# The start-up of a fused Fourier-mixing and gated-FFN kernel: even row sets first, half-width sums, merges last

## The chip, the cores and the metric

One core of a Trainium2 chip runs the whole kernel. The metric is the device time of one execution in microseconds, lower is better. The engines are TensorE (PE; its weight loads are listed as PEld), VectorE (DVE), ScalarE (ACT), GpSimd (POOL) and SyncE (SP), which issues the DMAs.

## The reference

```python
x = np.random.randn(8, 3008, 256).astype(np.float32) * 0.1     # batch, sequence, features
X = np.fft.fft(np.fft.fft(x, axis=1), axis=2).real.astype(np.float32)
t = X.reshape(8 * 3008, 256)                                    # tokens
gate = 1.0 / (1.0 + np.exp(-(t @ w_gate)))                      # w_gate, w_val: 256 x 1536
out = (gate * (t @ w_val)) @ w_out                              # w_out: 1536 x 256
```

The weights come as float64 and are made float32 on the chip.

## The kernel before

The Fourier transform over the sequence is matmuls with cosine and sine tables (`stab`); the one over the features is folded into the gate and value weights: `merge` multiplies a weight piece by the feature DFT table `dt` and leaves `G1` (cosines) and `G2` (sines).

**Rows.** A batch has 3008 rows. By symmetry four of them (`s`, `S - s`, `M + s`, `M - s`, with M = 1504) are folded into each other, so that 128 x 6 numbers `s = 6 p + q` remain: partition p, row set q from 0 to 5. `fold_ops` for batch 0 folds one entry of `SLICES` at a time on VectorE (lines 494 to 583: `point`, `first`, two `across`, two feature sums and a clear).

**Sums.** For batch 0, `half` sums over the six sets into two PSUM banks, `ev` (even q) and `od` (odd q), 377 or 376 columns wide: `blk` 0 are the even frequencies (NE = 377), `blk` 1 the odd ones (NO = 376). Cosines and sines each have both. `places` adds and subtracts `ev` and `od` into `pk` (cosines) and `qk` (sines), which the loop reads in chunks of 252 frequencies. `e_sums` does the same for one feature column (the "E" row), 1 partition wide; its result goes through DRAM (`ed`) and is read back by `e_rows` as `ek`, and its first chunk into `e0`.

**Loop.** For each batch, chunk and hidden tile, step i multiplies `G1` and `G2` with `pk` and `qk` into a PSUM bank `pf` (`front_a`, `front_b`), gates it (`gate_a`, `gate_b`: ScalarE and VectorE) and multiplies with `w_out` (`back`, banks `po`). Three banks of one pool serve `pf` and, in the start-up, sums and merges.

**Weights.** Piece j is loaded (`weight_load`), made float32 by `weight_parts` (ScalarE, lines 382 and 383) and `weight_join` (VectorE 392, 393, 395, then GpSimd 397), and merged by `weight_use` and `merge` (bank `ps`, copies at 417 and 418, small loads `ge` at 420). Pieces 0 and 1 are needed before the first step, 2 and 3 after the first `front_b`, and then one each step (5, 6, 8, ...).

**Order.** It is written out by hand: engines work through their instructions in the order in which the code issues them (`manual_schedule`). All SP loads share one queue; eight completion semaphores go round, so a load is issued when the one eight places before it has landed. Start-up in the code, from line 950: loads; parts and joins 0 and 1; warm-up matmuls on `dt`; merges 0 and 1; then for each slice the fold and the sums; placing; joins 2 and 3; the rest of the sine sums; then the loop. All matmuls are issued at line 133 and told apart by their tiles.

## Time and profile before

| | |
|---|---|
| median of three runs | 1909.43 us (1908.23 to 1909.88) |
| the profiled execution, its own time | 1909.15 us |
| its span in the profile | 1907.4 us |
| TensorE busy | 1895.6 us, 99% of the span |
| VectorE, GpSimd, ScalarE busy | 80%, 81%, 71% |
| granted TensorE clock | 1.00 |
| first `pf` weight load | 32.73 us after the start |

The profile is one execution: each row gives an engine's instructions by source line, with start or total, count and the time of one. "A <- B" names what an engine waited for. The chain of waits is followed back from the last instruction, at each step to what released it. Times in the text are microseconds from the start of the span.

### The profile page before, as it was taken

The page shows a single profiled execution, that of the slowest core. Times are in us where ns is not written, and L with a number is a line of the kernel's source. Part 1 is how long each engine was busy: PE and PEld are TensorE (multiplying, and loading weights), DVE is VectorE, ACT ScalarE, POOL GpSimd, SP SyncE. Part 2 cuts the span into 40 slices and gives each one's busy share as a digit, 9 for nine tenths or more (in the row PEclk, how much of TensorE's full clock was granted, in tenths as well). Part 3 has the DMA queues.
Part 4 walks back from the last instruction along what each step waited for, and adds up shares of the span by engine and source line. Part 5 has one row for each costly group of instructions (what it writes and reads, how often), then busy time and mean ns, then how long its engine had stood idle before and what let it go on. Part 6 is the DMA issues. An engine that isn't in the chain of part 4 may idle for free.

```text
span 1907.4 us, 36057 instructions
## 1 busy us (share of the span) xinstructions
PE 1895.6 (99%) x11836; PEld 1756.6 (92%) x11836; DVE 1520.6 (80%) x3375; ACT 1353.2 (71%) x3235; POOL 1543.4 (81%) x2733
## 2 busy tenths in 40 slices
PE   8999999999999999999999999999999999999999
PEld 5788999999999999999999999999999999999998
DVE  7678888878979778897788878888788777977775
ACT  4777777777777777777777777677767777777775
POOL 2489879987999779997799878999789986877770
PEclk9999999999999999999999999999999999999999
DMA  8446221212022121211211212122120110010001
GB/s 315 120 134 80 71 89 51 72 33 81 21 64 54 31 87 32 62 41 37 89 39 48 45 39 81 40 52 58 30 74 17 36 37 15 15 25 17 15 18 30
DMA packets 197333, 109.33 MB, mean 57 GB/s; under 512 B 134823, under 2 KB 188818, under 8 KB 195354
## 3 DMA queue, kind: packets, MB, share of 16 engines
q1 hardware_dynamic: 196568, 106.50, 21.1%
q8 instruction: 95, 1.56, 0.3%
q14 instruction: 92, 0.75, 0.1%
q10 hardware_dynamic: 546, 0.51, 0.1%
q0 software_dynamic: 32, 0.00, 0.0%
HBM read 71.24 MB, written 47.87 MB: 62 GB/s over the span
## 4 chain that ended last, share of the span: by engine, by line
PE 94%; DMA 2%; SPq 1%; POOL 1%; ACT 1%; DVE 0%; issue 0%; ACTq 0%; POOLq 0%
PE pf L133 49%; PE po L133 41%; PE sum L133 2%; DMA rtab<-in_stab_dram 1%; PE ps L133 1%; POOL sf L824 1%; DMA st<-in_stab_dram 1%; SPq L206 1%; DMA raw<-in_moe_w_val_dram 0%; PE od L133 0%; POOL x L507 0%; SPq L192 0%; SPq L375 0%; PE pe L133 0%; PE ev L133 0%
## 5 line engine op out<-in xcount | busy, mean ns | idle before, releaser
L824 POOL TENSOR_TENSOR sf<-h,sf 128x168 f32<-128x168 f32 (+1 forms) x1104 | 621.0, 582 | 79.5 <-DVE h L818 75.9
L824 POOL TENSOR_TENSOR sf<-h 128x168 f32<-128x168 f32 (+1 forms) x920 | 519.3, 584 | 159.8 <-DVE h L818 158.0
L133 PE MATMUL pf<-qk,G 128*128 128x252 f32 (+1 forms) x2304 | 583.4, 376 | 0.9 <-ACT ae L787 0.8
L133 PE MATMUL pf<-pk,G 128*128 128x252 f32 (+1 forms) x2304 | 582.7, 376 | 0.0
L772 ACT ACTIVATE pf<-ek,ge 128x252 f32<-128x252 f32 (+1 forms) x1142 | 538.2, 471 | 23.2 <-DMA ge<-G 3.0
L133 PE MATMUL po<-sf,wf 128*128 128x168 f32 (+1 forms) x2944 | 508.3, 305 | 0.0
L787 ACT ACTIVATE ae<-pf 128x504 f32<-128x504 f32 (+1 forms) x576 | 338.8, 588 | 218.7 <-PE pf L133 217.2
L133 PEld LDWEIGHTS pf<-pk,G 128*128 128x128 f32 x2304 | 435.9, 190 | 53.3 <-ACT pf L772 1.5
L133 PE MATMUL po<-h,wf 128*128 128x168 f32 (+2 forms) x2584 | 461.3, 307 | 0.0
L133 PEld LDWEIGHTS po<-sf,wf 128*128 128x128 f32 x2944 | 453.4, 190 | 8.0
L818 DVE TENSOR_TENSOR h<-pf,z 128x252 f32<-128x252 f32 (+1 forms) x576 | 240.4, 417 | 274.0 <-ACT pf L815 270.5
L802 DVE TENSOR_TENSOR z<-ae,pf 128x504 f32<-128x504 f32 (+1 forms) x576 | 384.6, 668 | 83.1 <-ACT h L801 79.1
L908 DVE TENSOR_TENSOR c<-c 128x168 f32<-128x168 f32 (+1 forms) x920 | 438.7, 500 | 3.3
L133 PEld LDWEIGHTS pf<-qk,G 128*128 128x128 f32 x2304 | 410.6, 190 | 32.3 <-ACT ae L787 2.1
L133 PEld LDWEIGHTS po<-h,wf 128*128 128x128 f32 x2584 | 410.4, 190 | 17.8 <-issue 0.9
L801 ACT ACTIVATE h<-pf 128x252 f32<-128x252 f32 (+1 forms) x576 | 216.9, 376 | 146.3 <-PE pf L133 129.0
L815 ACT ACTIVATE pf<-z 128x252 f32<-128x252 f32 (+1 forms) x576 | 214.3, 372 | 116.4 <-DVE h L814 114.5
L814 DVE TENSOR_TENSOR h<-h,pf 128x252 f32<-128x252 f32 (+1 forms) x576 | 232.9, 404 | 0.0
L824 POOL TENSOR_TENSOR sf<-sf 128x168 f32<-128x168 f32 (+1 forms) x184 | 101.7, 553 | 14.4
L824 POOL TENSOR_TENSOR sf<-sf,h 128x168 f32<-128x168 f32 (+1 forms) x184 | 110.1, 598 | 0.0
L891 ACT COPY c<-po 128x504 f32<-128x504 f32 (+1 forms) x138 | 78.5, 569 | 0.0
L918 DVE STREAM_TRANSPOSE os<-c 128x256 f32<-128x256 f32 x188 | 76.5, 427 | 0.1
(158 smaller groups left out, 876.4 us busy)
## 6 DMA issues: line engine op xcount, KB each, us to landing
x<-xr SPq DMA_DIRECT2D x14, 1536.0 KB
out_dram<-os SPq DMA_DIRECT2D x376, 56.0 KB
xr<-in_xf_dram SPq DMA_DIRECT2D x105, 128.0 KB
x<-x SPq DMA_DIRECT2D x112, 96.0 KB
xr<-in_xf_dram SPq DMA_DIRECT2D x14, 384.0 KB
ek<-ed SPq DMA_DIRECT2D x40, 126.0 KB
out_dram<-os SPq DMA_DIRECT2D x288, 7.0 KB
xr<-in_xf_dram SPq DMA_DIRECT2D x21, 124.0 KB
```

Source lines behind the costliest of these rows:

```text
L133: nc.tensor.matmul(o, l, r, start=start, stop=stop, skip_group_check=True)
L772: nc.scalar.activation(PF[i][:, g], EK[i // NFT], AF.Copy, scale=ge[:, g, f : f + 1])
L787: nc.scalar.activation(AP[i], PF[i], AF.Copy, scale=2.0)
L801: nc.scalar.activation(H[p][:, fh, 0:n], PF[i][:, 0], AF.Sigmoid)
L802: nc.vector.tensor_tensor(z[:, :, ::-1], AP.pop(i), PF[i], op=ALU.subtract)
L814: nc.vector.tensor_tensor(h[:, fh, 0:n], h[:, fh, 0:n], pf[:, 1], op=ALU.mult)
L815: nc.scalar.activation(pf[:, 0], z[:, 0], AF.Sigmoid)
L818: nc.vector.tensor_tensor(h[:, fh, n:], pf[:, 0], z[:, 1], op=ALU.mult)
L824: nc.gpsimd.tensor_tensor(block(p, dst), block(p, a), block(p, b), op=(ALU.subtract, ALU.add)[op])
L891: (nc.vector.tensor_copy if t == 1 or t == 3 else nc.scalar.copy)(C[0][:, 3 * t * R : 3 * (t + 1) * R], PO[t][:, 0 : 3 * R])
L908: nc.vector.tensor_tensor(t[:, dst * R : (dst + 1) * R], *v, op=(ALU.subtract, ALU.add)[op])
L918: nc.vector.transpose(os_[0][0][:, s, 0:nb, h, :], t[:, c0 : c0 + nb * TB])
```

## The change

- **Loads.** Row sets 4, 0, 2 come first, then 5, 1, 3. Sets 0 and 2 are mixed: even partitions of one go with odd partitions of the other, so each is loaded by two DMAs of 64 partitions (every second one). The tables of the even sets are loaded for 377 columns (H0 to H1) instead of 753, for sets 0 and 2 in the same mixed form (`load_mixed`), for set 4 into two zeroed pieces of `wf`, one with its even and one with its odd partitions (`load_apart`). `dt` moves from ScalarE's DMA queue to SP's, behind the rows; weight pieces 0 and 1 follow it. `load_again`, at step 35 of the loop, loads the cosine tables of the even sets whole, for the joint E sums of batches 1 to 7.
- **Sums.** With the sets mixed, all rows of one sum have the same sign under reversal of the frequencies. `seq_sums` makes two even sums x and y over half the columns, and `unfolded` gets all of them as x + y and, reversed, x - y. `e_first` does so for the E row, with ScalarE copies of y and the odd sums and its unfolded row in `ST[0]`.
- **Order.** `SLICES` are 4, (0, 2), 5, 1, 3. The warm-up is 8 matmuls on a zeroed piece of `wf`. Sums follow the folds; joins and merges of pieces 0 and 1 come after most odd sums, with pieces 2 and 3 behind them. `merge` gets its bank from its caller. The copy of `e0` moves from ScalarE to VectorE. `e_joint` holds what `e_sums` did for the other batches.

The diff, without removed helper bodies and blank lines:

```diff
@@ -188,11 +188,29 @@
     table = const.tile([2, 1], F32, name="table")
     ed = dram.tile([B, NK + 1], F32, name="ed")
-    def load_rows(q, n):
-        nc.sync.dma_start(out=X[0][0:NP, :, q : q + n], in_=xf[0, :, :, q : q + n])
-    def load_table(t, q, n, lo=0, hi=NE + NO):
-        nc.sync.dma_start(out=ST[t][0:NP, q : q + n, lo:hi], in_=stab[:, t, q : q + n, lo:hi])
+    def load_rows(*qs):
+        for q in qs:
+            for ps, r in ((slice(0, NP, 2), q), (slice(1, NP, 2), 2 - q)) if q in (0, 2) else ((slice(0, NP), q),):
+                nc.sync.dma_start(out=X[0][ps, :, q], in_=xf[0, ps, :, r])
+    H0, H1 = NE // 2, NE + NO // 2
+    def load_table(t, q):
+        nc.sync.dma_start(out=ST[t][0:NP, q], in_=stab[:, t, q])
+    def load_mixed(t):
+        for ps, qs in ((slice(0, NP, 2), slice(0, 3, 2)), (slice(1, NP, 2), slice(2, None, -2))):
+            nc.sync.dma_start(out=ST[t][ps, 0:3:2, H0:H1], in_=stab[ps, t, qs, H0:H1])
+    apart = [[wf[:, 2 * t + h].rearrange("p m n -> p (m n)")[:, 6 * WC : 6 * WC + NE] for h in range(2)]
+             for t in range(2)]
+    def load_apart(t):
+        for h in range(2):
+            nc.sync.dma_start(out=apart[t][h][h:NP:2], in_=stab[h::2, t, 4, H0:H1])
+    def load_again():
+        nc.sync.dma_start(out=ST[0][0:NP, 0:NQ:2], in_=stab[:, 0, 0:NQ:2])
     NQ4 = NE // 4 + 1
     TILES = [(g, par, par * HP + g * TB) for g in range(2) for par in range(2)]
@@ -405,11 +423,12 @@
         if w == 2:
             WO[c] = WS.pop(j)
         else:
-            merge(WS.pop(j), w, c, (4, 2, 3)[next(turns) % 3] if j > 1 else None)
-    def merge(ws, g, c, other):
+            merge(WS.pop(j), w, c, HELD.pop(j) if j in HELD else bank("ps", 2 + next(turns) % 3 if j else None))
+    HELD = {}
+    def merge(ws, g, c, ps):
         cs = slice(c * WC, (c + 1) * WC)
-        ps = bank("ps", other)
         for h in range(2):
             for t in range(2):
                 mm(ps[:, h * WC : (h + 1) * WC], dt[:, t, h * HD : (h + 1) * HD], ws[:, t, :],
@@ -482,7 +501,7 @@
     TURN = {}
     MORE = {}
-    SLICES = ((0, 1), (2, 3), (4,), (5,))
+    SLICES = (slice(4, 5), slice(0, 3, 2), slice(5, 6), slice(1, 2), slice(3, 4))
     def fold_ops(b, nq):
         x4 = X.pop(b)
@@ -581,7 +600,7 @@
                     nc.vector.tensor_tensor(to[:, :, :, 1:HD], v[:, :, :, 1:HD], v[:, :, :, D - 1 : HD : -1],
                                             op=op)
                 nc.vector.memset(r[:, :, :, 0:1], 0.0)
-            ops += [lambda q=q: half_rows(slice(q[0], q[-1] + 1)) for q in SLICES]
+            ops += [lambda q=q: half_rows(q) for q in SLICES]
         for blk, (v, r) in enumerate(parts):
             if b and blk:
                 W[b, blk] = v[:, :, HD:D], r[:, :, HD:D]
@@ -592,21 +611,49 @@
     PQE = {}
-    def half(b, w, d, blk, sn, other=None):
-        c0, n = ((0, NE), (NE, NO))[blk]
-        ev, od = [bank(name, other and other[i])[:, 0:n] for i, name in enumerate(("ev", "od"))]
-        def sums(*qs):
-            for q in sorted(qs, key=lambda q: q % 2):
-                mm((ev, od)[q % 2], w(q), ST[int(sn)][0:NP, q, c0 : c0 + n], q < 2, q >= NQ - 2)
-        def then():
-            a = evp.tile([P, NE], F32, name="a", tag="a")[:, 0:n]
-            nc.scalar.copy(a, ev)
-            return lambda: places(d, blk, sn, a, od)
-        return sums, then
+    def unfolded(f, x, y, sn=False):
+        nc.vector.tensor_tensor(f[:, H0:H1], x[:, 0:NE], y, op=ALU.add)
+        two = [t[:, 1:NE].rearrange("p (b n) -> p b n", b=2) for t in ((y, x) if sn else (x, y))]
+        nc.vector.tensor_tensor(f[:, 0 : 2 * H1].rearrange("p (b n) -> p b n", b=2)[:, :, H0 - 1 :: -1], *two,
+                                op=ALU.subtract)
+    def seq_sums(what, x, y, od):
+        d = PQE[0][what]
+        w = [W[0, blk][what] for blk in range(2)]
+        cols = (H0, NE - H0, 0), (NE, NO // 2, NE - H0)
+        turn = {}
+        def add(n, key, o, w, tab, first=True):
+            turn[key] = turn.get(key, 0) + 1
+            mm(o, w, tab, turn[key] == 1 and first, turn[key] == n)
+        def even(*qs):
+            for q in qs:
+                for blk, (lo, n, to) in enumerate(cols):
+                    for h in range(2):
+                        if q == 4 or h == q // 2:
+                            tab = apart[what][h][0:NP, to : to + n] if q == 4 else ST[what][0:NP, q, lo : lo + n]
+                            add(2, (h, blk), (x, y)[h][:, to : to + n], w[blk][:, q], tab, blk == 0)
+        def odd(q, *blks):
+            for blk in blks or range(2):
+                lo, n = ((0, NE), (NE, NO))[blk]
+                add(3, blk + 2, od[blk][:, 0:n], w[blk][:, q], ST[what][0:NP, q, lo : lo + n])
+        def copy():
+            a = evp.tile([P, NE], F32, name="a", tag="a")
+            nc.scalar.copy(a, y[:, 0:NE])
+            return a
+        def join(a):
+            f = hp.tile([P, 6 * WC], F32, name="u", tag="h") if what else wf[:, 0].rearrange("p m n -> p (m n)")
+            unfolded(f, x, a, what)
+            return lambda blk, *ends: places(d, blk, what == 1, f[:, blk * NE : NE + blk * NO],
+                                             od[blk][:, 0 : NE - blk], ends)
+        return even, odd, copy, join
     def places(d, blk, sn, ev, od, ends=(0, 1)):
         if 0 in ends:
@@ -691,53 +734,81 @@
-    E0 = []
-    def e_sums(m=B - 1):
...
+    def e_first():
+        ps = bank("pe")
+        cols = (H0, NE - H0, 0), (NE, NO // 2, NE - H0)
+        turn = {}
+        def add(n, band, blk, o, q, tab, first=True):
+            turn[band, blk] = turn.get((band, blk), 0) + 1
+            mm(ps[band * TB : band * TB + 1, o : o + tab.shape[1]], W[0, blk][2][:, q], tab,
+               turn[band, blk] == 1 and first, turn[band, blk] == n)
+                    if q % 2:
+                        lo, n = ((0, NE), (NE, NO))[blk]
+                        add(3, 2 + blk, blk, 0, q, ST[0][0:NP, q, lo : lo + n])
+                        continue
+                    lo, n, to = cols[blk]
+                    for h in range(2):
+                        if q == 4:
+                            add(2, h, blk, to, q, apart[0][h][0:NP, to : to + n], blk == 0)
+                        elif h == q // 2:
+                            add(2, h, blk, to, q, ST[0][0:NP, q, lo : lo + n], blk == 0)
+        def unfold():
+            er = op.tile([P, NK + 1], F32, name="er", tag="os")[0:1]
+            y, *o = (pool.tile([P, 2 * CH], F32, name=tag, tag=tag)[0:1, 0:NE]
+                     for pool, tag in ((zp, "z"), (zp, "z"), (app, "ae")))
+            for i, t in enumerate((y, *o)):
+                n = NE - i // 2
+                nc.scalar.copy(t[:, 0:n], ps[(i + 1) * TB : (i + 1) * TB + 1, 0:n])
+            f = ST[0][0:1, 4:6].rearrange("p q k -> p (q k)")
+            unfolded(f, ps[0:1], y)
+            def part(*ends):
+                for blk in range(2):
+                    places(er, blk, False, f[:, blk * NE : NE + blk * NO], o[blk][:, 0 : NE - blk], ends)
+                part(1)
+                nc.sync.dma_start(out=ed[0:1], in_=er)
+            part(0)
+            return er, end
+        return sums, unfold
     def e_joint():
...
@@ -950,68 +1021,87 @@
     nc.gpsimd.memset(nil, 0.0)
     nc.scalar.activation(table, nil[:, 0, 0:1], AF.Sigmoid)
     nc.gpsimd.dma_start(out=zero, in_=nil)
-    nc.scalar.dma_start(out=dt, in_=dtab.rearrange("(c p) d -> p c d", p=P))
     load_x(0)
-    for j in range(2):
-        weight_load(j)
-    load_rows(0, 2)
-    load_table(0, 0, 2)
-    load_rows(2, 2)
-    load_table(1, 0, 2, 0, NE)
-    load_table(0, 2, 2)
-    load_rows(4, 1)
-    load_table(0, 4, 1)
+    idle = wf[:, 0].rearrange("p m n -> p (m n)")[:, 0 : P + WC]
+    nc.vector.memset(idle, 0.0)
+    for t in apart:
+        for tab in t:
+            nc.gpsimd.memset(tab, 0.0)
+    load_rows(4, 0, 2)
+    for t in range(2):
+        load_apart(t)
+    for t in range(2):
+        load_mixed(t)
     load_rows(5, 1)
-    weight_load(2)
-    load_table(1, 2, 2, 0, NE)
-    load_table(0, 5, 1)
-    load_table(1, 4, 2, 0, NE)
-    load_table(1, 0, NQ, NE)
-    for j in (3, 5, 6, 8, 9, 4, 7):
+    load_table(0, 5)
+    load_rows(3)
+    load_table(0, 1)
+    load_table(1, 1)
+    nc.sync.dma_start(out=dt, in_=dtab.rearrange("(c p) d -> p c d", p=P))
+    weight_load(0)
+    load_table(0, 3)
+    weight_load(1)
+    load_table(1, 5)
+    load_table(1, 3)
+    for j in (2, 3, 5, 6, 8, 9, 4, 7):
         weight_load(j)
     e0 = shared["qk"][:, 4 * WC : 4 * WC + CH]
     nc.gpsimd.memset(e0, 0.0)
+    warm = bank("warm", 2)
+    for i in range(8):
+        mm(warm[:, 0:WC], idle[:, 0:P], idle[:, P:], True, True)
+    seq_start(0)
+    folds = iter(fold_ops(0, 2))
+    even, odd, copy, join = seq_sums(0, bank("u"), bank("u"), [bank("od", t) for t in range(2)])
+    e_, e_unfold = e_first()
+    od_s = [bank("od", 4)]
+    even_s, odd_s, copy_s, join_s = seq_sums(1, bank("u", 2), bank("u", 3), od_s)
+    for q in ((4,), (0, 2)):
+        next(folds)()
+        even(*q)
+        even_s(*q)
+    a, a_s = copy(), copy_s()
+    next(folds)()
+    odd(5)
+    e_(0, 2, 4, 5)
+    for f in folds:
+        f()
+    pk = join(a)
     weight_parts(0)
+    weight_join(0)
+    HELD[0] = bank("ps")
+    od_s.append(bank("od"))
+    odd(1)
+    odd_s(1, 1, 0)
+    e_(1, 3)
+    odd(3)
+    odd_s(5)
     weight_parts(1)
-    weight_join(0)
     weight_join(1)
-    warm = bank("warm", 2)
-    for i in range(4):
-        mm(warm[:, 0:WC], dt[:, 0, 0:P], dt[:, 0], True, True)
+    er, e_end = e_unfold()
+    weight_parts(2)
     weight_use(0)
+    odd_s(3, 1)
+    qk = join_s(a_s)
+    for blk in range(2):
+        pk(blk, 0)
+    nc.vector.tensor_copy(e0[0:1], er[:, 0:CH])
+    HELD[1] = bank("ps", 3)
     weight_use(1)
-    seq_start(0)
-    cos = [seq_group(0, blk, 0, (2 * blk, 2 * blk + 1)) for blk in range(2)]
-    e_, e_even = e_sums(1)
-    sin = [seq_group(0, 0, 1)]
-    for q, f in zip(SLICES, fold_ops(0, 2), strict=True):
-        f()
-        e_(*{1: (0, 1), 5: (2, 3, 4, 5)}.get(q[-1], ()))
-        sin[0][0](*{5: (3,)}.get(q[-1], ()))
-        cos[0][0](*q)
-        cos[1][0](*q)
-        sin[0][0](*{1: (0, 1), 4: (2,), 5: (4, 5)}.get(q[-1], ()))
-    places_c = [cos[blk][1]() for blk in range(2)]
-    weight_parts(2)
+    odd_s(3, 0)
     weight_join(2)
-    rest, *ends = e_even()
-    rest()
-    for f in ends:
-        f()
-    for f in places_c:
-        f()
-    nc.scalar.copy(e0[0:1], E0[0][:, 0:CH])
+    qk(0, 0)
+    qk(1, 0, 1)
     weight_parts(3)
     weight_join(3)
-    sin.append(seq_group(0, 1, 1, (0, 1)))
-    sin[1][0](*range(NQ))
+    qk(0, 1)
+    for blk in range(2):
+        pk(blk, 1)
+    e_end()
     for j in range(KEEP, KEEP + 3):
         weight_load(j)
-    places_s = [group[1]() for group in sin]
-    for f in places_s:
-        f()
     e_rows(0)
     per = NFT * len(chunks)
@@ -1043,6 +1133,7 @@
     for i, f in zip((1, 2, 2, 2, 3, 4, 4, 4, 5, 6, 6, 8, 8, 8, 9, 9, 9, 9, 10, 10, 10, 11, 11), quarter_x(1), strict=True):
         at(i, f)
     at(i0 + 1, lambda: load_x(1))
+    at(35, load_again)
     for b in range(1, B):
         at(20 + b, lambda b=b: e_load(b))
     at(3 * i0, e_fold)
```

## The prediction

> **What bounds the kernel now.** I read the page's totals, then the chain of waits, then the timeline of the first 60 us by engine.
>
> ```profile
> span 1907.4 us, 36057 instructions
> PE 1895.6 (99%) x11836; PEld 1756.6 (92%) x11836; DVE 1520.6 (80%) x3375; ACT 1353.2 (71%) x3235; POOL 1543.4 (81%) x2733
> ```
>
> TensorE is idle for 11.8 us in all. The chain of waits over the first 90 us says where:
>
> ```profile
> 14.43 9.31 DMA st<-in_stab_dram
> 23.74 0.04 issue
> 23.78 0.90 PE ev L133 x2
> ...
> 31.32 1.90 PE od L133 x6
> 33.21 4.25 PE pf L133 x20
> 37.46 3.45 PE ps L133 x16
> 40.91 0.90 PE pf L133 x4
> 41.81 1.73 PE ps L133 x8
> ```
>
> Up to 23.74 us the chain hangs on loads; from there on it is TensorE back to back. So the time is "when the loop's first steps start" plus a fixed amount of matmul, and the change touches only that start-up (after it, the instruction order is the same on every engine, apart from one reload). It can win at most a few us in 1909, and only if no later step then waits. The timeline gives durations:
>
> ```profile
> 7.48 1.29 POOL L397 TENSOR_TENSOR raw<-raw 128x512 int32<-128x512 int32 x1 [5.14 <-DVE raw L395]
> 7.84 1.22 DVE L392 TENSOR_SCALAR raw<-raw 128x512 f32<-128x512 f32 x1 [0.50 <-ACT raw L382]
> ...
> 19.49 0.68 DVE L494 TENSOR_TENSOR x<-x 128x510 f32<-128x510 f32 x1
> 22.01 0.68 DVE L494 TENSOR_TENSOR x<-x 128x510 f32<-128x510 f32 x1
> ...
> 30.06 0.53 DVE L617 TENSOR_TENSOR pk<-a,od 128x376 f32<-128x376 f32 x1
> 30.52 0.53 DVE L613 TENSOR_TENSOR pk<-a,od 128x376 f32<-128x376 f32 x1
> ...
> 38.81 1.70 PEld L133 LDWEIGHTS ps<-wqk,dt 128*128 128x128 f32 x8
> 40.69 0.72 PEld L133 LDWEIGHTS pf<-qk,G 128*128 128x128 f32 x4 [0.18 <-ACT ae L787]
> 41.44 1.70 PEld L133 LDWEIGHTS ps<-wqk,dt 128*128 128x128 f32 x8
> ```
>
> A fold of one row set takes 2.52 us (19.49 to 22.01), a placing operation 0.46 us (start to start), a weight join three VectorE operations (1.51) and one GpSimd addition (1.29, and 0.15 to be released). VectorE's L392, 1.22 us instead of 0.43, ended only after GpSimd's addition had: they lock each other out. The last row, the third merge in the loop (job 5), is my yardstick: 41.44.
>
> **The change, part by part.** All of it runs in the first 40 us.
>
> *Loads.* The DMA engines are full until 36 us, so a transfer lands when the bytes ahead of it have. From the trace's landings: a single row set 1.49 us (17.35 to 18.82, 19.83 to 21.34), a table set 1.0, a half table pair 1.06, a weight piece 1.35. The first transfer landed at 5.01; a row set put first, with 0.15 longer issue (0.61 for 0.46), I put at 5.3 (5.0 to 6.0). Then, bytes alone counting: four half transfers of row sets 0 and 2 to 8.3, four table parts for set 4 (0.27 each) to 9.3, four mixed table halves (0.53 each) to 11.5, sets 5 and 1 to 14.5, a table 15.5, set 3 to 17.0, two tables 19.0, the DFT table (0.75) 19.7, weight 0 at 21.1, a table 22.1, weight 1 at **23.4**, two tables 25.4, weight 2 at 26.8, weights 3 and 5 at 28.1 and 29.5. Dropped are three half tables for the sines and as many for the cosines, 1.16 MB or 3 us; what was 2-KB and 6-KB runs and is now 1-KB and 1.5-KB runs gives a third of that back.
>
> The twelve half transfers write every second partition, which no load of before does. Bounds: a full-partition stream runs at 386 GB/s, and 32-partition loads of the same 1.5-KB runs at 215:
>
> ```profile
> 24.00:33.00 9.00, 9.00 (x40) 4.65 (x40) 7.37 (x19) 5.26 (x11) 1.28 (x1) 1.00 1.06 386
> 140.00:144.00 4.00, 4.00 (x26) 3.82 (x26) 3.51 (x8) 3.44 (x9) 4.00 (x8) 1.00 1.07 215
> ```
>
> The last two columns of these stretches are the DMA engines' share and GB/s: equally busy, 1.8 times slower. The half transfers last 3.0 + 1.1 + 2.1 = 6.2 us at full rate, so the stretch costs 0 to 4.9 us. They span all 128 partitions, which is nearer to the first row, but two engines may meet at one place of the memory: I take 1.2 times, **+1.2 us**, and keep both ends.
>
> The Trainium skill (SBUF — State Buffer, "Door 1: The DMA port swizzle") says that the rate goes by how many of 16 ports the partitions reach, and that 64 neighbouring partitions do no better than 32. By its map alternate partitions reach all 16, so by the rule the stretch is nothing and the sum 1908.2. The 215 above agrees with its account of 32 partitions.
>
> At most eight transfers are out at once: each waits for the landing of the one eight before. At the tightest (the last mixed half) 2.6 us of bytes are still queued ahead, against some 1.9 us from issue to landing of a tiny transfer (ge, 43.13 to 45.04): no gap, but little to spare. GpSimd's four clears (0.34 for 252 columns) are done at about 4.0; the transfers that wait for them are needed at 8.3.
>
> *VectorE before the merges.* Fold 4 from 5.3 to 7.8, the mixed pair (4.11, as for a pair before) 8.3 to 12.4, sets 5, 1, 3 from the landing at 13.0 to 20.6. Fold work grows by 0.9 and the unfolding adds 6 operations, taken at the placing row's 0.46 (at most 0.67, L802's): the cosines' to 21.5. TensorE's even sums shrink (12 matmuls of 377 columns at 0.63 to 16 of 189); it waits for folds and tables there, so this saves nothing on the path.
>
> *Merges last.* The Abs of weight 1 (0.66) starts at its landing, 23.4; its join on VectorE starts at 24.1, is held by GpSimd's addition for weight 0 (23.4 to 24.7) and ends at 26.0; GpSimd's addition 26.15 to 27.4. Queued behind that join on VectorE are the E unfold, the sine unfold, all of pk and qk: this is the new wait. ScalarE copies E at 24.7 to 26.0; the E placings, now with both inputs in SBUF, are held until 27.4 and end at 28.4; sine unfold 29.3, pk (2 x 0.46) **30.25**. TensorE: od(3) after the table at 22.1, od_s(5) to 25.65, merge 0 (1.72) to 27.4, od_s to 28.0, merge 1 to 29.7, od_s to 30.35; G copied (0.37 + 0.38) by 30.6. Both let pf start at **30.4 against 32.73**, 2.3 earlier.
>
> *What then comes late.* VectorE from 30.25: e0 copy (0.06 to 0.40, I take 0.25), join 2 (1.51), three qk (1.4), join 3 (1.51) to 34.9, qk and two pk (1.4), two E ends (0.9), join 5 (1.51) to 38.7; with GpSimd 40.15. TensorE wants merge 5 after 20 pf records (4.25), two merges (3.45), one pf (0.85): 30.4 + 8.55 = 38.95. It waits 1.2 us, so merge 5 starts at **40.2 against 41.44**. Merges 2 and 3 are ready at 33.5 and 36.4, wanted at 34.7 and 36.4: just in time. Join 6 ends at 42.7, wanted at 43.7; gate work starts 1.6 later on VectorE than before, and pf(3), which needs its bank, has that to spare. SP issues the E row and three weight loads 0.5 later; they are used 12 us on.
>
> *Reload.* Step 35 reloads 1.16 MB of tables, issued near 171 behind stores, 0.8 us of SP and 3 us of transfer, about 177; the E matmuls (180.35 before) want it at about 179. The cover is 2 us; when it is gone, each us late costs one.
>
> **Sum.** -1.24 (merge 5) + 1.2 (half transfers, which move every VectorE step behind them) = 0.0, on the profiled run's 1909.15 us; its median of three is 1909.43, 0.3 higher. I predict **1909.4**.
>
> **Rivals.** *Slower: the half transfers run as the 32-partition rows do.* +4.9 instead of +1.2: 1909.4 + 3.7 = 1913.1. For it, the only partial-partition row; against, all partitions' range is reached. It decides from 1.2 times on (6.2 x 0.2 = 1.24). Chance 0.13. *Faster: full rate and VectorE not last.* If no lock hits and merge 5 is ready when wanted, the gain is pf's 2.3: 1907.1; with full rate and the wait as worked out, 1908.2 (in the forecast's range). Against: VectorE has 8.5 us of work between pk and join 5, without a gap. Chance 0.15. *The reload lands late*, as the E matmuls' new wait: 1909.4 plus up to 4, taken as 1911. The stretch at 160 to 180 has DMA engines a third busy, which speaks against. Chance 0.07. That the change doesn't do what it says is out: the built order shows the 16 short matmuls, the merges last and the reload.
>
> **How the numbers follow.** The forecast (1908.2 to 1911, stretch 1.0 to 1.45) has 0.60; 0.05 is left for something unseen. The range 1906.8 to 1913.2 takes in the faster rival less the runs' own spread, the first landing's bounds (-0.3 to +0.7), the unfold's (0 to +1.3) and most of the slower rival. 0.2% is 3.8 us, about what a measurement of this kernel can tell from no change: below 1905.6 needs more than pf's whole gain (0.03); above 1913.2 the upper half of the slower rival, and some of the reload and the unseen (0.12); between, 0.85.
>
> **What would show it.** In the profile after: row set 4's fold near 5.3; weight 1's Abs near 23.4 (full rate) to 24.6 (mine) or 28 (slow); the first pf near 30.4 to 31.6; an idle of about 1.2 us ahead of the third loop merge, released by GpSimd; no wait at the E matmuls near 179. Wrong I am if the first loads take much longer than their bytes, if the E placings or joins aren't held by GpSimd, or if TensorE idles after 45 us.

## The result

The changed kernel takes 1914.01 us (median of 11 runs, 1912.93 to 1914.59) against 1909.43 before (median of 11): a ratio of 1.0023, 95% interval 1.0014 to 1.0033. It is slower by 4.6 us, where 1909.4 was predicted and 1913.2 was the upper end. The profiled execution took 1913.42 us with a span of 1911.3, 3.9 above the span before.

The page's totals don't show where the time went: of the 3.9 us, TensorE's busy time has 2.7 and its idle time only 1.2. But 2.3 of the busy time is the longer warm-up (5.8 us of matmuls for 3.5), which runs while the first loads are still on their way, and part of the rest is matmuls at a lower clock (last section). What the change cost is read from where TensorE waits.

```profile
span 1911.3 us, 36139 instructions
PE 1898.3 (99%) x11856; PEld 1760.3 (92%) x11856; DVE 1528.1 (80%) x3390; ACT 1353.6 (71%) x3232; POOL 1546.9 (81%) x2737
```

### The profile page after: what moved, and what is told of

It reads as the page before. It is cut to its first block, busy times and chain, and to the rows that moved or that the text cites. A ratio compares the mean times of both kernels' runs of the same rounds, so it can differ in the third digit from the quotient of the medians.

```text
span 1911.3 us, 36139 instructions
## 1 busy us (share of the span) xinstructions
PE 1898.3 (99%) x11856; PEld 1760.3 (92%) x11856; DVE 1528.1 (80%) x3390; ACT 1353.6 (71%) x3232; POOL 1546.9 (81%) x2737
## 4 chain that ended last, share of the span: by engine, by line
PE 93%; SPq 2%; DMA 2%; DVE 1%; POOL 1%; ACT 1%; issue 0%; ACTq 0%; POOLq 0%; DVEq 0%
PE pf L133 49%; PE po L133 41%; PE sum L133 2%; DMA rtab<-in_stab_dram 1%; POOL sf L895 1%; SPq L224 1%; PE ps L133 1%; DMA st<-in_stab_dram 1%; PE od L133 0%; PE pe L133 0%; SPq L194 0%; POOL x L526 0%; SPq L265 0%; DVE c L979 0%; SPq L998 0%
## 5 line engine op out<-in xcount | busy, mean ns | idle before, releaser
L979 DVE TENSOR_TENSOR c<-c 128x168 f32<-128x168 f32 (+1 forms) x920 | 445.0, 507 | 3.3
L886 ACT ACTIVATE pf<-z 128x252 f32<-128x252 f32 (+1 forms) x576 | 214.5, 372 | 121.5 <-DVE h L885 118.7
```

Of the source, the lines that this page charges most:

```text
L886: nc.scalar.activation(pf[:, 0], z[:, 0], AF.Sigmoid)
L979: nc.vector.tensor_tensor(t[:, dst * R : (dst + 1) * R], *v, op=(ALU.subtract, ALU.add)[op])
```

## The profile after

The chain of waits over the first 60 us (start, length, what) answers to the chain shown of before.

```profile
0.74 0.72 SPq L194
...
4.18 0.61 SPq L210
...
10.05 0.63 SPq L194
10.68 0.04 issue
10.72 7.08 DMA st<-in_stab_dram
17.80 0.14 issue
17.93 1.58 PE od L133 x4
19.51 2.62 PE pe L133 x18
...
32.19 0.91 DVE pk L660 x2
...
41.92 1.40 DVE wf L411
...
43.95 0.67 DVE z L873
44.62 0.34 DVE h L885
...
45.05 0.38 ACT pf L886
45.43 0.59 ACT wf L400
46.02 0.56 ACT wf L401
46.58 0.25 ACT G L436
46.83 0.27 ACT G L437
47.10 0.04 issue
47.15 1.54 PE pf L133 x6
48.69 1.73 PE ps L133 x8
```

Read it in four pieces. Up to 10.7 us it is fifteen DMA issues of SP (SPq), back to back, each 0.52 to 0.72 us whether it moves 0.1 MB or 0.5. The sixteenth is a table, and its landing at 17.80 starts TensorE, which is dense from there to the first pf (33.46; 32.73 before). Then VectorE (DVE) is the chain, from pk without a gap to the gate of step 0, whose z comes at 43.95 (40.19 before). The last piece was not there before: ScalarE's sigmoid L886 waits for VectorE's h, behind it stand two weight parts (L400, L401), and behind those the two copies to G that pf(2) needs. Behind pf(2) comes merge 6 (job 6). Its weight loads, before first:

```profile
44.86 1.70 PEld L133 LDWEIGHTS ps<-wf,dt 128*128 128x128 f32 x8
```

```profile
48.32 1.70 PEld L133 LDWEIGHTS ps<-wf,dt 128*128 128x128 f32 x8
```

It starts 3.5 us later, most of the 3.9 of the span. (The chain's last row, 48.69, is a row of its matmuls; the expectations below set it against the weight loads' 44.86, which makes the loss 0.4 too large.)

TensorE's waits in the same stretch (us in total, times, longest) show where that is paid:

```profile
PE od L133 <- DMA st<-in_stab_dram: 2.2, 1, 2.2
...
PE pf L133 <- ACT G L437: 1.6, 1, 1.6
...
PE ps L133 <- POOL wqk L415: 0.5, 1, 0.5
```

The last row is the wait for merge 5 (43.08 against 41.44 before); its idle time was 0.9. So the 3.5 us are 0.7 of a later first pf, 0.9 ahead of merge 5 and 1.65 for the G copies, to within 0.3.

From 50 us on the two kernels run alike but for one wait near 150 us: ScalarE copies a table that has just landed, and TensorE waits for the `ae` behind that copy. It differs from run to run, 0 to 1.3 us in these kernels. Here are the kernel before, the changed one, and the run with seven full-width transfers (below):

```profile
PE pf L133 <- ACT ae L787: 0.6, 1, 0.6
```

```profile
PE pf L133 <- ACT ae L858: 0.5, 1, 0.5
```

```profile
PE pf L133 <- ACT ae L856: 1.3, 1, 1.3
```

The first copy of the last output chunk on ScalarE comes 3.6 us later than in the kernel before. These are the two rows, before first; I use them as a mark further on, and the wait near 150 us is in it.

```profile
1901.75 0.37 ACT L852 COPY c<-po 117x256 f32<-117x256 f32 x1 [4.17 <-PE po L133]
```

```profile
1905.37 0.37 ACT L923 COPY c<-po 117x256 f32<-117x256 f32 x1 [4.17 <-PE po L133]
```

And the loads are late in the middle of the start-up. The windows view (stretch, then busy times; the last two columns are the DMA engines' share and GB/s) shows them at 242 to 307 GB/s, where before moved 370 to 420:

```profile
8.00:10.00 2.00, 1.11 (x7) 1.14 (x8) 1.34 (x3) 0.00 (x0) 0.00 (x0) 1.00 0.92 255
10.00:12.00 2.00, 1.68 (x11) 1.39 (x9) 1.93 (x3) 0.00 (x0) 0.00 (x0) 1.00 0.87 242
12.00:14.00 2.00, 1.12 (x7) 1.12 (x8) 0.80 (x3) 0.00 (x0) 0.00 (x0) 1.00 0.97 307
14.00:16.00 2.00, 1.71 (x11) 1.42 (x9) 1.10 (x3) 0.73 (x2) 0.00 (x0) 1.00 1.00 298
```

Landings in the trace: set 5 at 14.84, set 1 at 16.80, its table 17.80, weight 0 at 23.36, weight 1 at 25.67.

Two theories came out of this: the loads are late (and three ideas why), and ScalarE's order turns VectorE's lateness into a wait of TensorE. The experiments take them in turn.

## Experiments: ScalarE's order

**Copies early.** In step 1 the merge of job 3, with its two G copies, is issued ahead of gate_b(0).

```diff
         for f in spare.pop(i, []):
             f()
+        if i == 1:
+            use[1].pop(0)()          # merge 3 and its copies
         if i:
             gate_b(i - 1, *join.pop(i, []), *between)
...
     (the code behind it, which issued this merge in step 1, no longer does)
```

> The changed kernel, but in step 1 the merge of job 3 (with its two copies to G on ScalarE) is issued ahead of gate_b(0) instead of behind it. TensorE's order stays the same; on ScalarE the two G copies stand ahead of the sigmoid of z(0) and of the weight parts of job 9, which wait for VectorE. Theory 2 (ScalarE's order: pf(2) waits 1.6 us only because its G copies stand behind a sigmoid that waits for VectorE): G is ready near 42, the 1.6 us ahead of pf(2) go and merge 6 starts near 47.1 (48.69): time about 1912.4. Rival (VectorE is simply late: something else of it, the bank of pf or the next join, ends last at the same place): the wait moves to another releaser and the time stays within 0.5 of 1914.

Measured: 1911.01 us (11 runs; ratio 1.0009, interval 1.0000 to 1.0017), 3.0 below the changed kernel. On ScalarE the copies now stand ahead of L886, and merge 6 starts at 46.54, 1.8 earlier:

```profile
41.82 0.37 ACT L436 COPY G<-ps 128x256 f32<-128x256 f32 x1 [0.31 <-PE ps L133]
42.09 0.38 ACT L437 COPY G<-ps 128x256 f32<-128x256 f32 x1
45.18 0.39 ACT L886 ACTIVATE pf<-z 128x252 f32<-128x252 f32 x1 [2.72 <-DVE h L885]
```

L886 still waits for VectorE and starts no sooner (45.18 for 45.05), but nobody waits for L886. That settles the 1.6 us; the order of TensorE's instructions is the same in both kernels. The mark stands at 1902.95, 2.4 us earlier than in the changed kernel; 0.5 of this is the wait near 150 us, which this run doesn't have.

**Ends late.** pk's and E's upper halves, with the E row's store and reload, go from ahead of the loop to the end of step 1.

```diff
-    for blk in range(2):
-        pk(blk, 1)
-    e_end()
...
+    at(1, lambda: (pk(0, 1), pk(1, 1), e_end(), e_rows(0)))
```

> The changed kernel, but the two upper placings of pk, the two E ends, the store of the E row and its reload (e_rows(0)) go from ahead of the loop to the end of step 1, behind joins 5 and 6 and the gate of step 0. That takes 1.86 us of VectorE work from ahead of join 5. Theory 3 (VectorE's queue): join 5 starts at 38.1 instead of 39.95, the 0.94 us ahead of merge 5 go, z(0) comes near 42.1, the G copies near 45.0, so that pf(2) waits 0.3 instead of 1.6: time down by about 2.2, to 1911.8. Rival (only ScalarE's order matters, and VectorE's lead is eaten by another wait): at most merge 5's 0.9, to 1913.1.

Measured: 1915.10 us (7 runs; ratio 1.0029, 1.0017 to 1.0040). That is 1.1 above the changed kernel, with intervals that overlap, and not the 2.2 below it that was forecast. Join 5 did start early (37.72), but ScalarE's second ae then waited for the gate of step 0, and TensorE 3.2 us for that ae:

```profile
43.35 0.59 ACT L858 ACTIVATE ae<-pf 128x504 f32<-128x504 f32 x1 [3.29 <-DVE z L873]
```

In the changed kernel this ae ran at 40.76 without a wait. The ae pool has two buffers, and one holds an E copy until the E ends have read it; with the ends moved, the second ae has to take the buffer of the first. That reading is argued from the code and the releaser; what speaks for it is that pk's ends moved alone (below), with the E ends left in place, bring no such wait.

**All three** (this, the copies early, and the two queues of the next section):

> The three edits together: half of the half transfers issued by ScalarE, the G copies of job 3 ahead of gate_b(0), and pk's and E's upper halves at the end of step 1. If the three causes are separate and are all there is: first pf near 31.3, no wait of TensorE over 0.3 us up to merge 6, which starts near 43.6 (44.86 in the kernel before, 48.69 in the changed one): time 1908.3, 1.1 below the kernel before. If weight pieces or joins of later jobs then end last (they land and are joined in a fixed time from the loads), merge 6 stays near 45 to 46 and the time near 1910.

1915.04 us: the ends' new wait (3.2 us ahead of qk(1)) covers whatever the other two bring. A bundle told nothing here.

**pk's ends alone late**, with the copies early, so that the buffer stays free:

> The run with the G copies of job 3 ahead of gate_b(0), and besides the two upper placings of pk (0.92 us of VectorE) go behind step 1's gate; the E ends stay where they are, so that ScalarE's second ae keeps its buffer. Theory: the 0.5 us that merge 5 still waited for GpSimd there go, and nothing takes its place: merge 6 near 46.2 (46.75 there), time about 1910.5 (1911.0). Rival: join 5 is no longer last, and its 0.5 us come back as a wait of another step, as in the run with all ends moved: 1911.0 or more.

1910.73 us (ratio 1.0008, 0.9999 to 1.0017), which cannot be told from 1911.01. The rival was right. VectorE lost 0.92 us of work ahead of join 5, but the E end that moved up fell on GpSimd's addition for job 3 (37.70 to 39.00) and took 1.46 us for 0.56:

```profile
37.95 1.46 DVE L664 TENSOR_TENSOR er<-st,z 1x376 f32<-1x376 f32 x1
```

Join 5 started at 39.79, and at 40.09 in the run it builds on, but pk had also ended 0.28 earlier here: from there to join 5 it is 6.92 us against 6.94. What is taken off VectorE's queue at this place comes back as time locked out by GpSimd.

## Experiments: the late loads

**Two queues.** The second transfer of each pair of halves is issued by ScalarE.

```diff
-                nc.sync.dma_start(out=X[0][ps, :, q], in_=xf[0, ps, :, r])
+                (nc.sync, nc.scalar)[i].dma_start(out=X[0][ps, :, q], in_=xf[0, ps, :, r])
     (likewise for the mixed tables and set 4's table parts)
```

> The changed kernel, but the second transfer of each pair of half transfers (row sets 0 and 2, set 4's table parts, the mixed table halves: six in all) is issued by ScalarE instead of SP. Bytes, partitions and order of use stay. Theory 1 (issue: SP needs 0.59 to 0.72 us for each transfer, small or large, and the DMA engines starve behind it): seven transfers instead of thirteen stand on SP ahead of set 5, so set 5 lands near 12.8 (14.84 in the changed kernel), weight 1 near 23.4 (25.67), the first pf starts near 31.3 (33.46), and the time falls by about 2.2, to some 1911.8 us. Rival (ports: writing every second partition is what is slow): landings within 0.3 us of those of the changed kernel, packets of the half transfers longer, time 1914 +- 0.5.

1912.75 us (1.0010 to 1.0027), an interval that overlaps the changed kernel's; the profiled execution took 1913.61. Set 1 landed at 16.80 and weight 1 at 25.68, within 0.01 us of where they had been. Theory 1 in the form "SP's issue is the limit" fell: with the issue halved, the ninth and later transfers waited for the landing of the one eight before (issued at 8.14 after a landing at 8.12), and DMA was at 228 GB/s from 8 to 10 us.

**Full width, half the count; full width, same count.** The halves become transfers over all partitions, seven in one kernel, thirteen of the old sizes in the other.

```diff
-   for ps, r in ((slice(0, NP, 2), q), (slice(1, NP, 2), 2 - q)): ... X[0][ps, :, q] <- xf[0, ps, :, r]
+   seven:    X[0][0:NP, :, q] <- xf[0, :, :, q]
+   thirteen: for hs in (slice(0, 2), slice(2, 4)): X[0][0:NP, hs, q] <- xf[0, :, hs, q]
     (tables likewise)
```

> The changed kernel, but each pair of half transfers is one transfer over all 128 partitions: seven transfers of the same bytes in place of thirteen, each with the same run lengths. Nothing is mixed by partition (odd partitions hold the set's own rows and set 4's two table parts aren't kept apart), so the sums over half the columns are other numbers; the instructions of the engines stay. Theory A (count: SP's 0.6 us for each transfer, and the eight that may be out at once, leave the DMA engines short of work) and theory B (writing every second partition stretches packets) both say that bytes bind again: set 5 lands near 12.7 (14.84), set 1 near 14.2 (16.80), weight 1 near 23.2 (25.67), no stretch below 340 GB/s between 7 and 16 us; first pf near 31.3, time near 1911.7. If landings stay as in the changed kernel, both fall and it is the 1024-byte runs themselves.

> As the full-width variant (nothing mixed, the sums over half the columns are other numbers), but with the thirteen transfers of the changed kernel: a row set in two transfers of two of its four blocks, a table set's columns in one transfer for each set, set 4's table columns in two halves of the columns (754-byte runs in place of 1508). All 128 partitions in each, the same bytes in each. Theory A (count) says as the changed kernel: set 5 near 14.8, set 1 near 16.8, weight 1 near 25.7. Theory B (alternate partitions) says as the full-width variant: set 1 near 14.2 to 14.6, weight 1 near 23.2.

Seven: set 1 at 14.82, weight 1 at 23.74, first pf 31.02, and from 8 us on:

```profile
8.00:10.00 2.00, 0.60 (x4) 0.63 (x5) 1.17 (x2) 0.00 (x0) 0.00 (x0) 1.00 1.05 381
10.00:12.00 2.00, 2.00 (x14) 1.90 (x12) 1.90 (x5) 0.00 (x0) 0.00 (x0) 1.00 1.08 378
```

Thirteen: set 1 at 14.97, weight 1 at 24.04. So it is not the count: the same number of transfers of the same bytes lands 1.6 us earlier when each covers all partitions. Theory B's forecast held to within 0.9 us, and so did the bytes' own schedule of the prediction (weight 1 at 23.4). One execution each took 1912.79 and 1911.62 us; merge 6 started at 46.11 and 46.43, 2.2 and 1.9 earlier than in the changed kernel, still behind 1.65 us for the G copies.

**Half blocks**, and the same read from every second row: partitions 0 to 63 and 64 to 127.

```diff
-   (slice(0, NP, 2), q), (slice(1, NP, 2), 2 - q)
+   (slice(0, 64), q), (slice(64, 128), 2 - q)      # rows 0:64, 64:128, or 0::2, 1::2 of the source
```

> The changed kernel, but the half transfers go to partitions 0 to 63 and 64 to 127, from neighbouring rows, instead of to every second partition; their number, bytes and run lengths stay, so do all instructions of the engines (the mixing is by half blocks, so the sums over half the columns are other numbers). Theory B1 (what costs 1.6 to 2 us in the changed kernel is that a transfer reaches only 64 partitions, of whatever kind): set 1 lands near 16.8 and weight 1 near 25.7 as there, or later by up to 3 if neighbouring partitions fare as the 32-partition stretch of the kernel before (215 GB/s). Theory B2 (it is the alternation, in the memory or in SBUF): as the full-width runs, set 1 near 15.0, weight 1 near 24.0.

> As the run with half blocks, but read from every second row of the source (DRAM), written to neighbouring partitions. It tells the two sides of the alternation apart: if reading every second row is what costs, set 1 lands 1 us or more later than in the half-block run; if writing to every second partition is, or the 64 partitions as such, it lands with the half-block run.

Set 1 landed at 17.28 and 16.72, weight 1 at 26.19 and 25.62. So it is as theory B1 has it, transfers to 64 partitions of either kind land late, and reading every second row costs nothing. Half blocks are slow in another way than alternate partitions: their 1024-byte packets took 82 ns (the median; 46 in both full-width runs), nearly all of them more than 60, at a steady rate with the engines busy:

```profile
8.00:10.00 2.00, 0.00 (x0) 0.00 (x0) 0.21 (x1) 0.00 (x0) 0.00 (x0) 0.84 1.12 245
```

In the changed kernel the usual packet is not stretched (46 and 65 ns for 1024 and 1508 bytes), but of those between 4 and 24 us, 83 took over 100 ns longer than usual, the longest 1.4 us; together 25 us, or 1.6 us for each of 16 engines. The kernel before has none, the full-width runs 20 and 35. This total does not follow the delay from run to run (15.9 us with two queues, 27.9 with set 5 early, for landings within 0.1), so that these packets are the delay is likely but not shown. And a transfer has landed when its slowest engine is done: for set 1 that was 2.35 us after the fastest (0.9 in the kernel before, 1.1 and 1.3 at full width).

The Trainium skill (SBUF — State Buffer, "Door 1: The DMA port swizzle") says that 64 neighbouring partitions reach half the ports; the half-block run agrees, with 82 ns for 46. By its map alternate partitions reach all ports; the usual packet agrees, the landings do not.

**Set 5 early; halves last.** Is it the empty queue at the head? Set 5 is loaded (and folded) second; then, in another kernel, all four full row sets go ahead of the halves.

```diff
-    load_rows(4, 0, 2)
+    load_rows(4, 5, 0, 2)          # and: load_rows(4, 5, 1, 3, 0, 2)
```

> The changed kernel, but row set 5 is loaded second, ahead of the half transfers, and folded second, ahead of the mixed pair; TensorE's order stays. The same transfers and bytes, twelve of them half, with 0.5 MB more in the queues when the short ones are issued. Theory C (empty queue: the short transfers carry 0.1 to 0.2 MB for 0.6 us of SP each, and at the head of the queue the DMA engines run out of work): no stretch below 330 GB/s up to 16 us, set 1 lands near 14.5 (16.80), weight 1 near 23.8 (25.67), first pf near 31.3 (33.46), merge 6 near 46.9 (48.69) behind the same 1.6 us for the G copies; time 1912.2. Theory B (writing every second partition is slow in itself): weight 1 within 0.4 of 25.7, time 1914.

> The changed kernel with its loads in another order only: the four full row sets (4, 5, 1, 3; 2 MB) first, then the same twelve half transfers, then the tables and weights as they were. The order of the engines' work stays, so the folds of the pair and all behind it wait for the later half sets and the time is not what this run is for. Theory C' (lead: a transfer that is issued less than some 3 us ahead of its turn leaves engines waiting; 2 MB ahead give the short ones 5 us of lead): each half row set lands 0.7 us after the last, no packet of the stretch from 4 to 18 us takes over 100 ns more than its size's usual time (83 in the changed kernel, none in the kernel before), and weight 1 lands near 23.6 (25.67). Theory B' (the half transfers slow what follows them, wherever they stand): the first table or two after them take 1 us or more too long, and weight 1 lands near 25.5 again.

1913.15 us (1.0012 to 1.0030) and, for one execution with all sums waiting, 1917.21. With set 5 ahead, the half row sets kept pace with their bytes (0.71 to 0.77 us each), but set 1 behind them then took 3.0 us instead of 1.5, and weight 1 landed at 25.75. With 2 MB ahead it was the first table behind them, 2.2 us instead of 1.0; weight 1 at 26.04, 88 long packets. Theories C and C' fell, twice: the delay moves with the half transfers and is paid at their end or just behind it.

What in the DMA engines makes those packets long is not settled. What is shown: twelve transfers to alternate partitions cost 1.6 to 2.3 us of landing time here, whoever issues them and in each of these three orders. With two weights and the DFT table ahead (next section) the cost was smaller: weight 2, behind the same bytes in another order, landed at 27.68 and 26.70 in two runs, 29.00 in the changed kernel, 27.05 and 27.37 at full width. The two runs have the same loads in the same order, so one execution can differ from the next by a us.

## Experiments: merges, sums, and the account

**Merges first.** Weights 0 and 1 and the DFT table are loaded, joined and merged first, as in the kernel before.

```diff
     load_x(0)
+    nc.scalar.dma_start(out=dt, ...)
+    for j in range(2): weight_load(j)
     load_rows(4, 0, 2)
...
     seq_start(0)
+    for f in weight_parts, weight_join, weight_use:
+        for j in range(2): f(j)
     (and the later parts, joins and uses of jobs 0 and 1 taken out)
```

> The changed kernel with one part undone: the DFT table and weights 0 and 1 are loaded first (the table by ScalarE's queue, as in the kernel before), and both pieces are joined and merged ahead of the folds. All other loads come in the changed kernel's order, some 3.4 us later: set 5 near 18.2, set 1 near 20.2, set 3 near 22.7, the last table near 27.6 as now. Theory (merges last: two joins, their waits for GpSimd and two merges stand between the last fold and the loop, on VectorE some 4.5 us, and it is this that makes join 5, the gate of step 0 and with it ScalarE's G copies late): TensorE has 11.6 us of sums from the table at 21.2, first pf near 32.8, merge 5 near 41.2 (43.1), wait for the G copies 0.5 or none (1.6), merge 6 near 45.2 (48.7), time 1909.6. Rival (the half transfers and late loads are the loss, and merging early only shifts it): time 1912 or more.

1912.63 us (1.0011 to 1.0028). A miss: pk came at 31.78, 0.3 earlier only, because the E unfold stands ahead of it on VectorE and waited for ScalarE's copies of the E sums:

```profile
28.80 0.54 DVE L615 TENSOR_TENSOR st<-pe,z 1x377 f32<-1x377 f32 x1 [2.54 <-ACT ae L770]
```

TensorE, ready early, waited 1.6 us for pk. Merge 5 (42.74) and the G copies (1.66) followed as in the changed kernel. So putting the merges first does not bring VectorE forward. What they cost alone this run can't say, since behind the two weights the folds ran later too (the last from 22.60; 19.91 in the changed kernel).

**Merges first, copies early, E sums early:**

> As the run with the merges first, and besides the G copies of job 3 ahead of gate_b(0) and the E sums of the even sets ahead of odd(5) on TensorE. If the G copies' 0.5 and TensorE's idle time ahead of odd(5) are what that run has left: first pf near 31.5, merge 5 set by VectorE and GpSimd near 40.9, merge 6 near 44.6, time 1909.0, a little below the kernel before. If VectorE's chain sets merge 5 later than that, 1909.6 as without them.

1911.65 us (1.0006 to 1.0024): the G wait is gone, pk later still (32.72), since the E sums moved ahead of odd(5) put off the later ones that the E copies wait for.

**Sums moved** (on pk's ends late): the even E sums ahead of odd(5), merge 0 ahead of odd_s(5).

> The run before it, and on TensorE the E sums of the even sets (about 2 us) go ahead of odd(5), into the 2.2 us that TensorE waits there for a table, and merge 0 goes ahead of odd_s(5), which waits for the sines' table of set 5 (26.66). Theory 4 (from 17.9 us on TensorE is dense up to the first pf, so that its own sums, not a load or VectorE, set that start): the first pf starts near 31.9 (33.5 to 33.9) and, as far as VectorE keeps up, merge 6 comes 1 to 1.6 earlier: time 1909.0 to 1909.6, level with the kernel before. Rival (VectorE's chain from the second join to join 5 sets merge 5 anyway): pf starts earlier but merge 5 waits the longer for it, time as the run before it.

1910.71 us, no change: first pf at 33.08 as in the run it builds on, merge 5 at 42.92, set by VectorE and GpSimd. Its rival was right: TensorE's start is not what decides.

**Set 5 early and copies early:**

> As the run before it, and the G copies of job 3 ahead of gate_b(0). If late loads and ScalarE's order are the whole loss, merge 6 starts near 45.0 (44.86 in the kernel before) and the time is 1909.5, level with the kernel before. If VectorE's chain of 11.8 us from pk to the gate of step 0, which is 2.6 longer in work than before, sets merge 5 whatever the loads do, then merge 5 stays near 42 to 43 and the time near 1910.5 to 1911.

1910.59 us (0.9999 to 1.0017), as with the copies alone; the loads were late as before (weight 1 at 25.91).

**Full width and copies early** takes both suspects away:

> The full-width variant (seven transfers over all partitions in place of thirteen, nothing mixed, so the sums over half the columns are other numbers), and the G copies of job 3 ahead of gate_b(0). It takes away both suspects at once, the late loads (weight 1 at 23.7 in place of 25.7) and ScalarE's order (1.65 us ahead of pf(2)). If these two are the whole loss: first pf near 31.1, merge 5 near 40.9, merge 6 near 44.7 (44.86 in the kernel before), time 1909.3, level with the kernel before. If VectorE's longer chain between pk and the gate of step 0 takes part of it back, merge 6 near 45.5 and 1910 or more.

First pf 30.48, merge 5 at 40.33, merge 6 at 43.65: 1.2 us ahead of the kernel before. The time is 1909.89 us against 1908.53 beside it (ratio 1.0007, 0.9998 to 1.0016), and the chain's end shows a loss that comes last:

```profile
1900.09 0.38 ACT c L921
1900.47 0.02 issue
1900.49 2.65 ACTq L922
1903.13 0.04 issue
1903.18 0.37 ACT c L921
```

The mark is at 1900.09, 1.66 us earlier than before, but the last store but one took ScalarE 2.65 us to issue, 0.59 in the kernel before, and SP's next store came later too. In both kernels SP had issued a store 1.24 us ahead of it. Six of the variants (both full-width ones, both half-block ones, halves last, this one) have this and need 7.0 to 7.3 us from the mark to the end; the kernel before needs 5.6, the changed one 5.9, so it has no part in the changed kernel's loss. Five of the six ran once only: whether the kernel or the execution triggers it is not shown.

The account at merge 6 (its weight loads, in us against the kernel before, 44.86): changed kernel +3.5; without ScalarE's order +1.7; without the half transfers +1.6 (thirteen) or +1.3 (seven); without both (seven) -1.2. So ScalarE's order costs 1.8 with the half transfers and 2.5 without them (1.3 to -1.2), and the half transfers cost 1.9 to 2.2 with that order and 2.9 without it (1.7 to -1.2). The terms overlap, each partly hidden behind the other, and together they are 4.7, more than the loss: without them the change is worth its 1.2 us at this point. By the mark the same runs stand at +3.6, +1.2, +1.0, +2.0 and -1.7; the wait near 150 us makes most of the difference, 1.3 us of it in the seven full-width transfers. Each of these figures comes from one profiled execution, and the 11 times of the changed kernel lie 1.7 us apart, so a term is good to about 1 us. Besides, TensorE's clock stayed at 1.00 in the full-width runs while it fell in the changed kernel and in the copies-early one (last section), so about 0.5 of the half transfers' price may be the clock's. None of the kernels beats the one before.

## Why the prediction was wrong

Point by point, by its own steps.

- *Loads by bytes*: right. Weight 1 at 23.4 was forecast for full rate; the full-width run has 23.74.
- *Half transfers +1.2*: mis-sized, and for another reason. The landings came 1.6 to 2.3 later, weight 1 at 25.67 for my 24.6, and at merge 6 it measured 1.9 to 2.9. I priced a stretch of every packet; the usual packet isn't stretched, 83 stall.
- *"No gap, but little to spare"*: failed. DMA ran at 242 to 255 GB/s from 8 to 12 us. I had counted the eight outstanding transfers but not SP's 0.6 us for each transfer, which stands in the chain from 0.74 to 10.72. Taking that away alone brought nothing, so it is not the cause by itself.
- *First pf at 30.4 (31.6 with the stretch)*: 33.46. The table of set 5 landed at 17.80 for my 16.7, and TensorE was dense from there for 15.5 us; at full clock it needs 15.0, close to the 14.9 in my figures. The other 0.5 is the clock (last section). That TensorE itself is the chain there I had not seen: I wrote that it waits. It is not alone, for with its sums moved forward the first pf stayed at 33.08, since VectorE's pk came no earlier (31.96 and 31.97).
- *Join 1 and the E placings held by GpSimd*: right, L410 1.02 us and L660 0.89 in place of 0.41 and 0.53.
- *VectorE's queue from pk to join 5*: right, 8.45 forecast, 33.02 to 41.47 measured. Since pk ended 1.6 later than I had it, so did merge 5 (43.08 for my 41.4 with the stretch), its wait 0.9 for 1.2.
- *"Gate work starts 1.6 later ... pf(3), which needs its bank, has that to spare"*: the step that failed. z came 3.8 later than before (43.95 for 40.19), where 1.6, or 2.8 with the stretch, was forecast, and the one who had nothing to spare was pf(2), through two G copies that stand behind that gate in ScalarE's queue. I followed the data (which bank, which tile) but not the queue of the third engine, and so the sum has nothing for this wait. It was 1.65 us long and cost 1.8 us at merge 6 with the half transfers in place, 2.5 without them; taking it away won 3.0 us of time. With it the sum is no longer -1.24 + 1.2 but, at merge 6, -1.2 for the change, 1.9 to 2.9 for the half transfers and 1.8 to 2.5 for ScalarE's order: +3.5 in all. My own sign for being wrong, TensorE idle after 45 us, is this wait, which ended at 47.15.
- *Reload*: right, TensorE waits no longer at the E matmuls near 184 us than in the kernel before (0.13). My row of the kernel before was read too low: its DMA engines are 59% busy from 160 to 170 us and 33% from 170 to 180; it had no consequence.
- *Rivals*: the slower one (1913.1) came near the time but not by its way: the half transfers took 1.6 to 2.3 us of landings of their possible 4.9, and the rest is ScalarE's queue. The faster one did not show: with both costs gone, merge 5 still waited 1.4 us for GpSimd. That run is the sum's own full-rate case, first pf 30.48 for 30.4, merge 5 40.33 for 40.2, and 1.2 us won at merge 6 for 1.24.

## What to carry to other kernels

When a step gets later, list for every engine what stands behind it in that engine's queue, not only who uses its result: here two copies that had long been ready to run waited behind a sigmoid. Work that is taken off a full VectorE queue can come back as time locked out by GpSimd (all of 0.92 us here), so price such a cut with the neighbour's operations in view. And load over all partitions: the transfers that touch every second partition look free by their usual packet and still landed 1.6 to 2.3 us late here. Loading whole rows and mixing them on the chip was not tried.

## What the runs showed that I had not expected

- A DMA issue took SP 0.52 to 0.72 us in the changed kernel's first fifteen, whether it moved 94 KB or 512 KB; the same pieces over all partitions (thirteen transfers) took 0.33 to 0.47 but for the first two, 0.71 and 0.60.
- Alternate partitions: unstretched packets, and 83 stalls of up to 1.4 us.
- TensorE's granted clock fell to 0.50 near 19 to 22 us in the changed kernel, after 2.2 us of idle time. So it did for a while between 9 and 23 us in six more of the runs, and in the other ten it stayed at 1.00 over that stretch, once after 1.9 us of idle time at the same place (ends late) and once after 2.4 (pk's ends alone). The row is the changed kernel's:

```profile
20.00:22.00 2.00, 2.00 (x18) 0.70 (x14) 1.90 (x5) 0.00 (x0) 0.00 (x0) 0.50 1.07 383
```

The E sums of that stretch took 2.62 us for 1.39. The Trainium skill (TensorE: Matmul & The Clock Gate, "Part 1: The HAM clock gate") has the half clock after an idle window of some 3.4 us and the full clock after a busy one, with windows that run free of the kernel. That the fall lasted 3.41 us here (19.23 to 22.65; twice that in a half-block run) agrees; that 2.2 us of idle time were enough does not, and the measurement decides. In these traces the granted clock changes in steps of 3.41 us, counted from a start that differs from run to run; a fall followed each such stretch in which TensorE was idle for 2.04 us or more (nine cases) and none with 1.84 or less. So the same idle time tells or not by how it falls on these stretches.
- A store that ScalarE issues at the very end, 1.24 us after one of SP, took it 2.63 to 2.65 us in six variants and 0.58 to 0.63 in the others.
